# Smaller halves of a second fold by integer sum and difference on GpSimd, in 30 slots of a top-k attention and mixture-of-experts kernel

## The chip, the cores and the metric

The kernel runs on one core of a Trainium2 chip. The metric is device time in microseconds (us) of one execution; three executions of the kernel before gave 1314.14, 1318.43 and 1321.39, median 1318.43. The engines are named as in the profile: PE is TensorE, PEld its weight loads, DVE VectorE, ACT ScalarE, POOL GpSimd, SP the queue that issues most transfers.

## What is computed

Attention over 8 batches with 8 heads, 576 positions and head size 64, where each query keeps only its 32 best keys; then a mixture of experts with one expert out of 8 per token. All is float32.

```python
scores = scale * np.matmul(q, k.transpose(0, 1, 3, 2))
kth = np.partition(scores, -32, axis=-1)[..., -32:-31]
scores = np.where(scores >= kth, scores, -1e9)
...
attn = attn / (np.sum(attn, axis=-1, keepdims=True) + 1e-09)
x = np.matmul(attn, v)            # then heads side by side: 4608 rows of 512
...
h = np.maximum(x_sorted[lo:hi] @ w1[e], 0.0)
y_sorted[lo:hi] = h @ w2[e]
y = gate_w[:, None] * y[inv_perm]
```

## The kernel before

**Slots.** The attention goes in 144 slots, 18 to a batch. A slot holds two tiles of 128 query rows with 576 scores each, so 2 x 576 elements per partition. `loop()` writes out the order of PE, ACT and DVE by hand, slot after slot. Scores are made three to four slots ahead (`AHEAD`), so PE and ACT may lag behind DVE by some slots before it starves. Transposes and the product with V follow a slot later, and pieces of the expert blocks, planned by a credit that counts slots and not time, fill PE in between. From the first token rows that are ready (slot 25 on) expert blocks come in; what is left of them after the last slot is done by PE alone at the end.

**The search on DVE.** For the 32nd largest score of a row, DVE does not search all 576. `fold` (L313, L315) takes the larger and the smaller of column c and column c + 288: `h` and `l`. `fold_on` (L321, L323) does it again with `h`: the larger of each two go to `few[0:144]`, the smaller to `hl`, 144 wide. `search` first takes the eight largest of `l` and of the two halves of `hl` (L352, six MAX8 for two tiles) and puts them behind the 144 in `few`, which is then 168 wide. Four rounds then each take the eight largest (L361) and, but for the last, strike them out (L369). The first round needs the first 144 columns only. Round 0 strikes out in place in `few`; later ones write to `scr`. The order in DVE's queue in slot i is: `h` and `l` for slot i+1 (two-input TENSOR_TENSOR), the six lists for slot i, rounds 0, 1 and 2, then `few` and `hl` for slot i+1, then the last round. `h`, `hl` and `scr` have one buffer each, `few` three, `l` two.

**What follows it.** ACT turns the threshold into `low` (L378) and into `w` (L394); POOL subtracts (L403, two instructions for a slot), then writes a check value, `doubt` (L384); ACT takes the exponent (L411). Earlier in the slot, after round 0, POOL makes the bias of that exponent, `nbias` (L365). POOL works in order: L403 and L384 of slot i-1 come before L365 of slot i. In some slots it also scales finished rows (L496 to L509), scatters them (L574) or stores expert rows (L841), the last two as indirect transfers.

Of the kernel before, what the change touches and what calls it, by code (L numbers as in the profile page):

```python
# [9 lines left out]
F32 = mybir.dt.float32  # L10
I32 = mybir.dt.int32
AF = mybir.ActivationFunctionType
ALU = mybir.AluOpType
# [31 lines left out]
def kernel(  # L45
# [47 lines left out]
    nc = tc.nc  # L93
# [40 lines left out]
    def open_pools(st, exact):  # L134
        for name, bufs in (
            ("load", 2), ("att", 2), ("xp", 1 if exact else 2), ("small", 2),
            ("wp", 1 if exact else 2), ("mlp", 2),
        ):
            setattr(k, name, st.enter_context(tc.tile_pool(name=name, bufs=bufs)))
        for name, bufs in (("ps_s", 2), ("ps_t", 2), ("ps_m", 2)):  # L140
            pool = tc.tile_pool(name=name, bufs=bufs, space=bass.MemoryType.PSUM)
            setattr(k, name, st.enter_context(pool))
        k.exact = exact
        k.apart = k.between = False

    def load_unit(b, u, parts=False):
        n = SimpleNamespace(b=b, u=u)
# [167 lines left out]
        nc.vector.tensor_tensor(f.l, s[:, :, 0, :], s[:, :, 1, :], op=ALU.min)  # L315
        return f

    def fold_on(f):

        f.few = k.att.tile([P, 2, LW], F32, name="few", bufs=3)  # L320
        nc.vector.tensor_tensor(f.few[:, :, 0:QF], f.h[:, :, 0:QF], f.h[:, :, QF:HF], op=ALU.max)  # L321
        f.hl = k.att.tile([P, 2, QF], F32, name="hl", bufs=1)
        nc.vector.tensor_tensor(f.hl, f.h[:, :, 0:QF], f.h[:, :, QF:HF], op=ALU.min)  # L323

    aside = []

# [10 lines left out]
        if steps in aside:  # L337
            aside.remove(steps)

    def search(tiles, s, f, then=lambda: None):  # L340

        m_all = range(2)
        tops = k.small.tile([P, 2, TOP_K], F32, name="tops", bufs=4)
        if k.exact:
            src = [s[:, m, :, :].rearrange("p j k -> p (j k)") for m in m_all]
            width = S
        else:
            src = [f.few[:, m, 0:QF] for m in m_all]
            width = LW
            for m in m_all:  # L350
                for j, away in enumerate((f.l[:, m, :], f.hl[:, m, 0:QF // 2], f.hl[:, m, QF // 2:QF])):
                    nc.vector.max(out=f.few[:, m, QF + 8 * j:QF + 8 * j + 8], in_=away)  # L352
        scr = k.att.tile([P, 2, width], F32, name="scr", bufs=1)
        nbias = k.small.tile([P, 2], F32, name="nbias", bufs=3)
        R = TOP_K // 8

        for r in range(R):
            if r == R - 1:
                then()
            for m in m_all:  # L360
                nc.vector.max(out=tops[:, m, r * 8:(r + 1) * 8], in_=src[m])  # L361
                if r > 1:
                    tick()
            if r == 0:
                in_turn(nc.gpsimd.tensor_scalar_mul(nbias, tops[:, :, 0], -scale))  # L365
            if r < R - 1:
                for m in m_all:
                    first = r == 0 and not k.exact
                    nc.vector.match_replace(  # L369
                        out=src[m] if first else scr[:, m, :], in_to_replace=tops[:, m, r * 8:(r + 1) * 8],  # L370
                        in_values=src[m], imm_value=NEG,
                    )
                    if r > 1:
                        tick()
                    src[m] = f.few[:, m, :] if first else scr[:, m, :]
        thr = tops[:, :, TOP_K - 1]
        low = k.small.tile([P, 2], F32, name="low", bufs=3)
        nc.scalar.activation(low, thr, AF.Copy, scale=STEEP)  # L378

        def doubts():  # L380
            n, i = tiles[0]
            at = n.b * U + n.u
            over = doubt[:, at:at + 2, 2 * NC, :] if tails(tiles) else doubt[:, at, 2 * i:2 * i + 2, :]
            k.last_pool = in_turn(nc.gpsimd.tensor_tensor(  # L384
                over, f.few[:, :, QF + 7:LW:8], _inner(thr, NL), op=ALU.subtract
            )).ins

        return low, nbias, doubts
# [113 lines left out]

    def rows(n, x):

        rzb = rz_of[n.u % 2][:, :].rearrange("p (t h) -> p t h", h=2)
        at = 0 if n.u % 2 else lw
        xu = x[:, :, n.u * P:(n.u + 1) * P].rearrange("p t (h d) -> p t h d", h=2)
        xl = n.xl[:, :, at:at + P].rearrange("p t (h d) -> p t h d", h=2)
        in_turn(nc.gpsimd.tensor_tensor(xu, xl, _inner(rzb, D), op=ALU.mult))  # L509
# [453 lines left out]
    FIRST = 13  # L963
    ARRIVED = 13
    AHEAD = 3
    ON_CHIP = 3
    KEEP = 3 * PIECES
    BETWEEN = 2

    with fast:  # L970
# [39 lines left out]

        def put_stores():
            while stores:
                stores.pop(0)()

        def following():
# [29 lines left out]
        def scatter(n):  # L1045
            nonlocal left
            for _ in range(min(n, len(scatters))):
                scatters.pop(0)()
            if not scatters and coming:
                waiting.extend(coming)  # L1050
                left += len(coming) * PIECES
                coming.clear()
                ahead()
# [121 lines left out]
        def loop():  # L1175
            nonlocal credit, rate, clock
            for i in range(min(AHEAD, len(work))):
                multiply(i)
                s_of[i], steps = scores(got_of.pop(i))
                for step in steps:  # L1180
                    step()
            multiply(AHEAD)
            f_of[0] = fold(s_of[0])
            fold_on(f_of[0])
            for i, (b, g) in enumerate(work):
                tiles = tiles_of(i)
                u, tile = g[0]
                if tile == 0 and u % 2 == 0:
                    open_unit(tiles[0][0])
                if tails(tiles):  # L1190
                    open_unit(tiles[1][0])

                then = lambda: None
                if i + 1 < len(work):
                    f_of[i + 1] = fold(s_of[i + 1])
                    then = lambda: fold_on(f_of[i + 1])
                low, nbias, doubts = search(tiles, s_of[i], f_of.pop(i), then)
                at_place("small")
                w_of[i] = depths(s_of[i], low)
                less(s_of.pop(i), w_of[i])  # L1200
                doubts()
                at_place("pool")
                at_place("relu")
                at_place("rows")
                put_stores()
                scatter(1)
                at = i % per_batch
                if at == FIRST and b:
                    rate = level(b) * PIECES / (U * NT)
                credit += rate * len(g)  # L1210
                room = left
                if b == B - 1 and at >= ARRIVED:
                    room -= KEEP
                    credit = room / (len(work) - i)
                share = {0: 0.5, 1: 1.2, 2: 1.6, 3: 0.5, 2 * NC: 1.4}[tile]
                now = max(0, min(int(credit * share + 0.5), room))
                credit -= now
                clock = i
                if i + AHEAD < len(work):
                    s_of[i + AHEAD], steps = scores(got_of.pop(i + AHEAD))  # L1220
                    for step in steps:
                        step()
                evacuate()
                at_place("turn")
                turns = turning(i - 1) if i else iter(())
                next(turns, None)
                part = min(BETWEEN, now - now // 2)
                rest = pieces(part)
                next(turns, None)
                rest = pieces(now - now // 2 - part + rest)  # L1230
                weights(tiles, w_of[i], nbias)
                next(turns, None)
                evacuate()
                if i + AHEAD + 1 < len(work):
                    multiply(i + AHEAD + 1)
                if tile == NC - 1:
                    end = ending(b, u)
                    late.append([end, next(end)])
                at_place("products")
                at_place("weights")  # L1240
                credit = min(credit + pieces(now // 2 + rest), 6 * rate)

            k.between = True
            for _ in turning(len(work) - 1):
                pieces(1)
            assert len(late) == 1
            clock = None
            for place in late[0][0]:
                if place == "rows":
                    pieces(4)  # L1250
            kept = left - (SURE + HALVES + PLAIN) * PIECES
            assert kept >= 0, kept
            k.apart = True
            pieces(kept)
# [136 lines left out]
```

## Time and profile before

| what | value |
|---|---|
| the profiled execution's own time | 1319.47 us |
| its span | 1317.9 us, granted PE clock 0.965 |
| median of three runs | 1318.43 us (1314.14 to 1321.39) |
| busy, share of the span | PE 90%, DVE 81%, ACT 71%, POOL 50% |
| L403 on POOL | 288 instructions, 1434 ns each, 405.5 us idle before them |
| L323 on DVE (`hl`) | 144 instructions, 463 ns each |
| L321 on DVE (`few`) | 144 instructions, 550 ns each |
| mean device memory traffic | 168 GB/s |

A group's row gives the line, the engine, the operation, what it writes and reads, the count, then busy time and mean duration, then the idle time just ahead of it and who ended that. A timeline row gives start and duration in us; a bracket at its end is the idle time before it. Busy tenths are in 40 equal slices of the span, some 33 us each. On DVE an instruction's duration overlaps the next one by some hundredths, so the step from start to start says what it costs in a full queue.

### The profile page before, as it was taken

To read this page: it belongs to the slowest core of one execution; us is meant where nothing else is said; L and a number is where in the kernel's file an instruction comes from. 1 tells how busy PE (TensorE), PEld (TensorE's weight loads), DVE (VectorE), ACT (ScalarE), POOL (GpSimd) and SP (SyncE) were. 2 spreads that over 40 slices of the span, in tenths; PEclk is the share of its full clock that TensorE was granted. 3 is DMA by queue.
4 is the path that set the end of the run, shared out by engine and by line. 5 is a ranking of instruction groups with operands and counts; after the bars stand their busy time and mean duration, and the time that the engine had idled before them with its cause. 6 is when DMAs were issued, how large, how long until landed. Compare 5 with 4: busy or idle time off the path is not lost. (4 is left out here: it accounts for less than half of the span.)

```text
span 1317.9 us, 24504 instructions
## 1 busy us (share of the span) xinstructions
PE 1191.3 (90%) x7654; PEld 836.6 (63%) x7654; DVE 1069.2 (81%) x4617; ACT 931.7 (71%) x2136; POOL 662.0 (50%) x807
## 2 busy tenths in 40 slices
PE   5676777899889989999999999999999999999995
PEld 3343444655566556666666666667666777699973
DVE  8999999999999999999999999999999942000000
ACT  4788877888888887888788887898878851111110
POOL 2454546455755574658564745576558642000000
PEclk9788878999999999999999999999999999999998
DMA  4001013741473147434855554447454549986670
GB/s 149 29 30 30 30 38 102 267 161 39 137 265 140 46 156 282 174 110 148 299 173 182 166 210 173 165 150 292 145 204 149 205 154 311 378 284 212 212 291 18
DMA packets 98508, 220.94 MB, mean 168 GB/s; under 512 B 5181, under 2 KB 25917, under 8 KB 98368
## 3 DMA queue, kind: packets, MB, share of 16 engines
q1 hardware_dynamic: 91664, 199.02, 43.8%
q0 software_dynamic: 6416, 19.97, 4.2%
q8 instruction: 62, 1.02, 0.3%
q14 instruction: 78, 0.64, 0.2%
q10 hardware_dynamic: 288, 0.30, 0.1%
HBM read 195.88 MB, written 24.17 MB: 167 GB/s over the span
## 5 line engine op out<-in xcount | busy, mean ns | idle before, releaser
L403 POOL TENSOR_TENSOR w<-s,w 128x576 f32<-128x576 f32 x288 | 407.3, 1434 | 405.5 <-ACT w L394 405.4
L926 PE MATMUL ph<-xTs,w 128*128 128x128 f32 x2112 | 262.9, 279 | 5.1 <-ACT xTs L823 3.0
L926 PEld LDWEIGHTS ph<-xTs,w 128*128 128x128 f32 x2112 | 251.3, 194 | 24.3 <-issue 20.5
L943 PE MATMUL py<-w,hT 128*128 128x512 f32 x528 | 248.3, 599 | 3.9 <-ACT hT L931 3.7
L411 ACT ACTIVATE w<-w,nbias 128x576 f32<-128x576 f32 x288 | 224.1, 793 | 2.9 <-POOL w L403 2.2
L394 ACT ACTIVATE w<-s,low 128x576 f32<-128x576 f32 x288 | 207.6, 768 | 4.7
L299 PE MATMUL sc<-qkb 64*128 64x288 f32 (+1 forms) x1280 | 200.2, 463 | 9.4 <-ACT s L306 5.1
L422 PE MATMUL wTm<-turn,w 128*128 128x128 f32 x1152 | 166.9, 284 | 22.8 <-ACT xl L477 11.0
L422 PEld LDWEIGHTS wTm<-turn,w 128*128 128x128 f32 x1152 | 130.4, 144 | 79.7 <-issue 33.6
L306 ACT COPY s<-sc 128x576 f32<-128x576 f32 x288 | 168.7, 639 | 10.3 <-PE sc L299 10.3
L1270 DVE CAST any_i<-pd 1x1 int32<-1x1 f32 x1 | 0.1, 146 | 205.4 <-PE pd L1268 205.4
L361 DVE MAX8 tops<-scr 128x8 f32<-128x168 f32 x576 | 165.4, 315 | 0.0
L429 ACT COPY wT<-wTm 128x512 f32<-128x512 f32 x256 | 138.9, 603 | 23.8 <-PE wTm L422 23.7
L299 PEld LDWEIGHTS sc<-qkb 64*128 64x128 f32 (+1 forms) x1280 | 107.5, 191 | 70.0 <-issue 31.4
L361 DVE MAX8 tops<-few 128x8 f32<-128x144 f32 (+1 forms) x576 | 151.0, 300 | 0.0
L459 PE MATMUL po<-wT,vb 128*64 128x288 f32 x1024 | 150.0, 439 | 0.0
L943 PEld LDWEIGHTS py<-w,hT 128*128 128x128 f32 x528 | 91.9, 191 | 88.5 <-issue 82.6
L352 DVE MAX8 few<-l 128x8 f32<-128x288 f32 x288 | 127.1, 441 | 0.0
L841 POOL DMA_INDIRECT out_dram<-y,xg x37 | 38.9, 1052 | 173.5 <-ACT y L952 88.1
L459 PEld LDWEIGHTS po<-wT,vb 128*64 128x64 f32 x1024 | 72.5, 147 | 72.9 <-issue 21.6
L313 DVE TENSOR_TENSOR h<-s 128x576 f32<-128x576 f32 x144 | 109.3, 759 | 2.0 <-ACT s L306 2.0
L315 DVE TENSOR_TENSOR l<-s 128x576 f32<-128x576 f32 x144 | 108.6, 754 | 0.0
(188 smaller groups left out, 1654.5 us busy)
## 6 DMA issues: line engine op xcount, KB each, us to landing
w<-in_moe_w_dram SPq DMA_DIRECT2D x74, 2048.0 KB, 9.2
qkb<-in_qk_dram SPq DMA_DIRECT2D x31, 608.0 KB, 3.9
vb<-in_v_dram SPq DMA_DIRECT2D x32, 320.0 KB, 3.2
xg<-x_rows SPq DMA_DIRECT2D x37, 257.0 KB, 9.3
x_rows<-blank SPq DMA_DIRECT2D x13, 257.0 KB, 5.7
x_rows<-blank POOLq DMA_DIRECT2D x4, 257.0 KB, 9.7
x_rows<-x,posi POOLq DMA_INDIRECT x40, 3.5
out_dram<-y,xg POOLq DMA_INDIRECT x37, 4.1
```

Source lines behind the costliest of these rows:

```text
L299: nc.tensor.matmul(ps[rows, j, 0:HF], n.q[d, cols], n.k[d, keys], start=True, stop=True)
L306: lambda m=m, ps=ps: nc.scalar.copy(s[:, m, :, :], ps[:, :, 0:HF]) for m, ps in enumerate(got)
L352: nc.vector.max(out=f.few[:, m, QF + 8 * j:QF + 8 * j + 8], in_=away)
L361: nc.vector.max(out=tops[:, m, r * 8:(r + 1) * 8], in_=src[m])
L394: nc.scalar.activation(w[:, m, :], s[:, m, :, :].rearrange("p j k -> p (j k)"), AF.Relu, scale=-STEEP, bias=low[:, m:m + 1],)
L403: k.last_pool = in_turn(nc.gpsimd.tensor_tensor(w[:, m, :], s[:, m, :, :].rearrange("p j k -> p (j k)"), w[:, m, :], op=ALU.subtract)).ins
L411: nc.scalar.activation(w[:, m, :], w[:, m, :], AF.Exp, scale=scale, bias=nbias[:, m:m + 1], accum_out=n.z[:, c:c + 1])
L422: nc.tensor.transpose(pm[:, c * P:(c + 1) * P], w[:, m, first:first + P], ident)
L429: nc.scalar.copy(wT[:, :, m, q], pm4)
L459: nc.tensor.matmul(po[r, 0:HF], n.v[:, c, r], rhs, start=(c == 0), stop=(c == KC - 1))
L926: nc.tensor.matmul(ph[:, f, :], n.w1[:, 0, dt, fc * P:(fc + 1) * P], n.xT[:, dt, :], start=(dt == 0), stop=(dt == DT - 1),)
L943: nc.tensor.matmul(py, hT[:, f, :], n.w2[:, 0, f, :], start=(f == 0), stop=(f == FT - 1))
```

## The change

`fold_on` gets a second way to make `hl`: read as integers, the smaller of two numbers is their sum less the larger, and this is exact on the bits whatever they stand for. Two POOL instructions on int32 views (sum, then difference) take the place of one DVE minimum. It is used where a slot is "quiet": numbers 1 to 47, if no row scaling, scatter or store was queued since the last search. In the built program that is slots 1-7, 9-11, 13-16, 18-20, 22-24, 31-34, 36-38 and 40-42, that is 30. There `few` for the next slot comes already after round 1's maxima, ahead of round 1's strike-out, and POOL's two instructions stand in its queue behind `nbias` and ahead of L403 of the same slot. In a slot whose `hl` came from POOL the six lists come after round 0 instead of ahead of it.

```diff
-    def fold_on(f):
+    def fold_on(f, aside_too=False):
         f.few = k.att.tile([P, 2, LW], F32, name="few", bufs=3)
         nc.vector.tensor_tensor(f.few[:, :, 0:QF], f.h[:, :, 0:QF], f.h[:, :, QF:HF], op=ALU.max)
-        f.hl = k.att.tile([P, 2, QF], F32, name="hl", bufs=1)
-        nc.vector.tensor_tensor(f.hl, f.h[:, :, 0:QF], f.h[:, :, QF:HF], op=ALU.min)
+        hl = k.att.tile([P, 2, QF], I32, name="hl", bufs=1)
+        f.hl, f.aside = hl[:, :, :].bitcast(F32), aside_too
+        if aside_too:
+            one, other, more = (a.bitcast(I32) for a in (f.h[:, :, 0:QF], f.h[:, :, QF:HF], f.few[:, :, 0:QF]))
+            in_turn(nc.gpsimd.tensor_tensor(hl, one, other, op=ALU.add))
+            in_turn(nc.gpsimd.tensor_tensor(hl, hl, more, op=ALU.subtract))
+        else:
+            nc.vector.tensor_tensor(f.hl, f.h[:, :, 0:QF], f.h[:, :, QF:HF], op=ALU.min)
...
+    def lists(f):
+        for m in range(2):
+            for j, away in enumerate((f.l[:, m, :], f.hl[:, m, 0:QF // 2], f.hl[:, m, QF // 2:QF])):
+                nc.vector.max(out=f.few[:, m, QF + 8 * j:QF + 8 * j + 8], in_=away)
...
-            for m in m_all:
-                for j, away in enumerate(...)
+            if not f.aside:
+                lists(f)
...
-            if r == R - 1:
+            if r == R - 1 and not soon:
                 then()
...
+            if r == 1 and soon:
+                then()
...
+                if first and f.aside:
+                    lists(f)
...
+    QUIET = 48
...
-                then = lambda: None
+                then, quiet = lambda: None, 0 < i < QUIET and not k.crowded
                 if i + 1 < len(work):
                     f_of[i + 1] = fold(s_of[i + 1])
-                    then = lambda: fold_on(f_of[i + 1])
-                low, nbias, doubts = search(tiles, s_of[i], f_of.pop(i), then)
+                    then = lambda: fold_on(f_of[i + 1], quiet)
+                low, nbias, doubts = search(tiles, s_of[i], f_of.pop(i), then, quiet)
+                k.crowded = False
```

`k.crowded` is set to true where rows are scaled, stores are put out and rows are scattered.

More of the change, by code (lines that the diff above doesn't have):

```diff
@@ L143, in open_pools @@
         k.exact = exact
-        k.apart = k.between = False
+        k.apart = k.between = k.crowded = False
     def load_unit(b, u, parts=False):
@@ L338, in through, with search @@
             aside.remove(steps)
-    def search(tiles, s, f, then=lambda: None):
+    def lists(f):
+        for m in range(2):
+            for j, away in enumerate((f.l[:, m, :], f.hl[:, m, 0:QF // 2], f.hl[:, m, QF // 2:QF])):
+                nc.vector.max(out=f.few[:, m, QF + 8 * j:QF + 8 * j + 8], in_=away)
+    def search(tiles, s, f, then=lambda: None, soon=False):
         m_all = range(2)
@@ L349, in search @@
             width = LW
-            for m in m_all:
-                for j, away in enumerate((f.l[:, m, :], f.hl[:, m, 0:QF // 2], f.hl[:, m, QF // 2:QF])):
-                    nc.vector.max(out=f.few[:, m, QF + 8 * j:QF + 8 * j + 8], in_=away)
+            if not f.aside:
+                lists(f)
         scr = k.att.tile([P, 2, width], F32, name="scr", bufs=1)
@@ L503, in rows @@
     def rows(n, x):
+        k.crowded = True
         rzb = rz_of[n.u % 2][:, :].rearrange("p (t h) -> p t h", h=2)
@@ L1012, in put_stores @@
             while stores:
+                k.crowded = True
                 stores.pop(0)()
@@ L1047, in scatter @@
             for _ in range(min(n, len(scatters))):
+                k.crowded = True
                 scatters.pop(0)()
```

## The prediction

> **What bounds the kernel now.** First the busy tenths, since the change touches only the first 48 slots of 144, that is up to 354 us by the timeline.
>
> ```profile
> PE   5676777899889989999999999999999999999995
> ...
> DVE  8999999999999999999999999999999942000000
> ```
>
> DVE is full to slice 32, PE only from about slice 9 on. Next the busy time by stretches of 50 us:
>
> ```profile
> 50.00:100.00 50.00, 36.27 (x216) 21.35 (x216) 50.00 (x217) 42.01 (x101) 26.29 (x34) 0.86 0.12 39
> ...
> 300.00:350.00 50.00, 43.73 (x305) 28.77 (x302) 50.00 (x225) 41.66 (x101) 32.59 (x38) 1.00 0.18 59
> ...
> 1150.00:1200.00 50.00, 50.00 (x297) 46.75 (x296) 0.00 (x0) 7.84 (x13) 2.88 (x3) 1.00 0.73 252
> ```
>
> The numbers are PE, PEld, DVE, ACT, POOL. Up to 350 us DVE has no idle time at all and PE, ACT and POOL do. So a microsecond off DVE's queue there is a microsecond off the kernel, if nothing else becomes late. Afterwards PE binds, in an order fixed by slot; it starts from where DVE left it (up to slot 69, at 505 us, ACT still waits for DVE at nearly every `low`), so a lead made by slot 47 should last to the end. The chain of waits names no engine for the body and is of no use here.
>
> Then one slot on DVE, the one whose `h` starts at T = 80.72:
>
> ```profile
> 79.88 0.44 DVE L323 TENSOR_TENSOR hl<-h 128x288 f32<-128x288 f32 x1
> 80.24 0.56 DVE L361 MAX8 tops<-scr 128x8 f32<-128x168 f32 x2
> 80.72 0.73 DVE L313 TENSOR_TENSOR h<-s 128x576 f32<-128x576 f32 x1
> ...
> 84.28 0.55 DVE L361 MAX8 tops<-few 128x8 f32<-128x168 f32 x2
> ```
>
> And on POOL:
>
> ```profile
> 81.93 2.83 POOL L403 TENSOR_TENSOR w<-s,w 128x576 f32<-128x576 f32 x2 [3.75 <-ACT w L394]
> 84.72 0.20 POOL L384 TENSOR_TENSOR doubt<-few,tops 128x6 f32<-128x6 f32 x1
> 84.89 0.21 POOL L365 TENSOR_SCALAR nbias<-tops 128x2 f32<-128x2 f32 x1
> 89.42 2.79 POOL L403 TENSOR_TENSOR w<-s,w 128x576 f32<-128x576 f32 x2 [4.32 <-ACT w L394]
> ```
>
> POOL is idle from 85.10 to 89.42, and the next `h` starts at 87.71. A slot without other small work lasts 6.92 us from `h` to `h`, all of it DVE's.
>
> **Removed.** 30 L323. The row says 463 ns, but start to start (79.88 to 80.24) it costs 0.36. 30 x 0.36 = 10.8 us, the ceiling of the gain; 30 x 0.46 = 13.9 counts overlap twice.
>
> **Added on POOL.** An int32 TENSOR_TENSOR of 2 x 144 is nowhere in the trace. L403 (float32, 576) takes 1.41 in its median, L498 (40 elements) 0.27: on that line 288 take 0.80. Lower bound 0.68 (L509, 640 in 1.26, whose second input is broadcast), upper bound 1.41 (L403 whole, were integers twice as slow). I take 0.80, its nearest row in kind, so 1.6 plus about 0.08 between the two, as L498 and L499 show between dependent ones. The rule against this: the Trainium skill, GPSIMD Engine Reference, section "Engine selection", keeps elementwise work on VectorE, as GpSimd is about twice as slow with two inputs. The rows agree (1.41 against 0.73 for 576). Were POOL on the path, 30 x (1.68 - 0.36) = 40 us would be lost; the trace has POOL idle 4.3 us here, so by the row the two are hidden. That cover decides.
>
> **Who waits for them.** L403 of the slot is queued behind them: needed 1.2 us after the next T, so free. DVE's next `h` overwrites what the sum reads: done in time. The strike-out of round 0 now waits for the difference (it overwrites `few`): due 1.75 after the next T, so free; an extra semaphore at about 0.02 (the EVENT_SEMAPHORE row's 21 ns) makes 0.6 us in all. The lists wait for `hl` still later. That they and the maxima change places moves nothing on DVE's sum.
>
> **What moves: `few`, by 1.7 us.** This is where cost arises. A second view shows what happens when a two-input DVE instruction meets POOL:
>
> ```profile
> 515.79 2.79 POOL L403 TENSOR_TENSOR w<-s,w 128x576 f32<-128x576 f32 x2 [6.71 <-ACT w L394]
> 518.53 0.43 POOL L384 TENSOR_TENSOR doubt<-few,tops 128x6 f32<-128x6 f32 x1
> ```
>
> DVE at the same time:
>
> ```profile
> 517.40 1.50 DVE L321 TENSOR_TENSOR few<-h 128x288 f32<-128x288 f32 x1
> 518.82 0.45 DVE L323 TENSOR_TENSOR hl<-h 128x288 f32<-128x288 f32 x1
> ```
>
> `few` stood from 517.40 to 518.90, 1.06 longer than its 0.44, until POOL's subtraction was over. The Trainium skill, SBUF — State Buffer, section "Who interferes with whom", has it so: a VectorE instruction with two SBUF inputs and a GpSimd instruction that reads SBUF exclude each other for a whole instruction. MAX8 and MATCH_REPLACE rows, with one input, show no such stretch. Before, `few` came at 86.50, T + 5.78, clear of L403's end at T + 4.04. Now it comes when round 1's maxima end: 84.28 + 0.48, T + 4.04, in the very moment. On-time slots: at best no wait; at worst it stands behind `doubt` and `nbias`, 0.35. As the pending DVE instruction goes first in the view above (`doubt` is stretched, not `few`), I take 0.1: 24 x 0.1 = 2.4 us.
>
> Late slots: where ACT is behind, L403 ends later. In slot 11 (T = 87.71) `low` is not preceded by idle time, L403 ends at T + 4.50, and with ACT's slack cut by 0.3 a slot at T + 4.8: `few` loses 0.7. Doing this for every quiet slot (ACT's work from `low` to `low` less its idle time, against the shorter slot) gives 0.25, 0.3, 0.45 and 0.25 in slots 15, 24, 34 and 42. In slot 40 row scaling left over from slot 39 holds L403 until T + 5.49: `few` can slip in between its two instructions, but then the difference runs into the next `h`, about 0.7. Together 2.7 us.
>
> **Does POOL get done?** From the start of `few`, DVE goes 2.52 us to the next `h` (0.37 + 0.60 + 0.47 + 0.60 + 0.48). POOL needs the rest of `few` 0.4, `nbias` 0.25, sum and difference 1.68, less some 0.1 at the end: 2.23. It fits with 0.29 to spare, which allows 0.94 an instruction.
>
> Sum: -10.8 + 0.6 + 2.4 + 2.7 = -5.1. The profiled execution's 1319.5 becomes 1314.4. That execution is 1.0 above the median, so in runs 1313.3.
>
> **Rivals.**
> 1. *Integers are slow* (slower). The place is the next `h`, held by the difference. Each 0.1 over 0.94 an instruction costs 0.2 a slot; from about 1.12 on that eats the 0.36. A stalled `h` gives L403 the lead it lacked, so `few`'s waits are left out. At the bound, 1.41, `h` waits 0.93: (0.93 - 0.36) x 30 + 0.6 = +18, 1336; at 1.27 it waits 0.65: +9, 1328, which I take. Against it: 128-lane rows with two inputs lie on one line whatever they do. 15%.
> 2. *No collisions*: `few` wins the tie and ACT, which waits inside its slots for PE too, keeps up. -10.8 + 0.6 = -10.2: 1308. 22%.
> 3. *POOL wins the tie*: `doubt` and `nbias` go ahead each time, 0.25 in 24 slots: -10.8 + 0.6 + 6.0 + 2.7 = -1.5: 1317. 15%.
> 4. *The lead is lost behind slot 47*, PE's work from 520 us on having its own pace. Against it: ACT's waits for DVE up to slot 69. 1318. 8%.
>
> My own case has 40%.
>
> **The numbers.** 0.5% is 6.6 us, about what a measurement of this kernel can tell from no change. Faster by more: rival 2 and 30% of my case, 0.34. Slower by more: rival 1 mostly, 0.13. Within: 0.53. The range: 1308 (rival 2) to 1321 (my case and rival 3 with the 2.6 us by which the runs of before stand from their median on either side, and short of rival 1).
>
> **What would show it.** L323 on DVE x114; two new POOL groups x30 near 800 ns (over 1100: rival 1); L313 unstretched in slots 1 to 47 (median 0.73); L321's total up by about 4.4 us, its mean from 550 to about 580 ns; ordinary quiet slots of 6.6 to 6.7 us in place of 6.92; and slot 48's `h` at about 349, not 354. If slot 48 comes early and the end does not, rival 4 holds.

## The result, and the profile after

The changed kernel takes 1313.03 us in the median of 18 runs (1311.18 to 1316.37), the kernel before 1318.64 in 18 (1314.14 to 1321.65). The ratio is 0.996, with a 95% interval of 0.9951 to 0.9968: by the ratio 5.3 us faster, between 4.2 and 6.5. The medians here and below leave out two executions that ran in a far slower state, one of the kernel with the minimum left out (1725.94 us, granted PE clock 0.651) and one of the kernel before (1730.48 us). Forecast were 1313.3 and a gain of 5.1 us, so the size came out to within a tenth of a per cent of the whole. By its steps the forecast was less good: one cost that it counted is not there, and another is larger.

The page of the changed kernel, its busy tenths:

```profile
PE   5776676899889989999999999999999999999995
...
DVE  7999999999999999999999999999999943000000
ACT  4888877898888888988888887898878851111210
POOL 4777766777755575658564745576558542000000
```

DVE is still full, and POOL's slices two to eight have gone from four to six tenths to six or seven. By stretches of 50 us (PE, PEld, DVE, ACT, POOL):

```profile
50.00:100.00 50.00, 37.16 (x225) 22.52 (x225) 49.76 (x210) 43.05 (x103) 36.48 (x46) 0.86 0.12 39
300.00:350.00 50.00, 43.95 (x308) 29.68 (x306) 49.91 (x220) 42.54 (x101) 38.30 (x41) 1.00 0.20 64
...
1150.00:1200.00 50.00, 50.00 (x318) 49.45 (x318) 0.00 (x0) 9.44 (x15) 2.72 (x3) 1.00 0.75 266
```

In the first of these POOL is busy for 36 us where it was for 26. The groups that answer to the rows of before (POOL's new pair, `few`, the minimum that is left on DVE, the check value):

```profile
L321 DVE TENSOR_TENSOR few<-h 128x288 f32<-128x288 f32 x144 | 80.8, 561 | 0.0
...
L329 DVE TENSOR_TENSOR hl<-h 128x288 f32<-128x288 f32 x114 | 53.3, 467 | 0.0
...
L399 POOL TENSOR_TENSOR doubt<-few,tops 128x6 f32<-128x6 f32 x144 | 45.4, 315 | 0.0
...
L327 POOL TENSOR_TENSOR hl<-hl,few 128x288 int32<-128x288 int32 x30 | 24.4, 815 | 2.4
L326 POOL TENSOR_TENSOR hl<-h 128x288 int32<-128x288 int32 x30 | 23.8, 794 | 0.0
```

The integer instructions take 794 and 815 ns, against 800 forecast from the float32 rows. `few` is only 11 ns longer in the mean; `doubt` is 63 ns longer (it took 36.3 us in all before). How that comes shows in an ordinary slot, T = 24.41. POOL:

```profile
25.62 2.83 POOL L418 TENSOR_TENSOR w<-s,w 128x576 f32<-128x576 f32 x2 [1.41 <-ACT w L409]
28.41 0.54 POOL L399 TENSOR_TENSOR doubt<-few,tops 128x6 f32<-128x6 f32 x1
28.92 0.21 POOL L378 TENSOR_SCALAR nbias<-tops 128x2 f32<-128x2 f32 x1
29.09 0.79 POOL L326 TENSOR_TENSOR hl<-h 128x288 int32<-128x288 int32 x1
29.97 0.80 POOL L327 TENSOR_TENSOR hl<-hl,few 128x288 int32<-128x288 int32 x1
```

and DVE:

```profile
28.45 0.44 DVE L321 TENSOR_TENSOR few<-h 128x288 f32<-128x288 f32 x1
28.81 0.08 DVE L382 MATCH_VALUE_LOAD scr<-tops,few 128x8 f32 x1
...
30.96 0.74 DVE L313 TENSOR_TENSOR h<-s 128x576 f32<-128x576 f32 x1
```

`few` starts 0.04 after `doubt` and takes its bare 0.44; it is `doubt` that stands, 0.54 in place of 0.20. So the tie goes to DVE, at no cost, and in no ordinary quiet slot of this profile is `few` stretched. The difference ends at 30.77, 0.19 ahead of the next `h`. The slot lasts 6.55 us, not 6.92: 0.37 less, all of the step that was removed.

A late slot is number 6, T = 50.62. POOL, then DVE:

```profile
53.14 2.76 POOL L418 TENSOR_TENSOR w<-s,w 128x576 f32<-128x576 f32 x2 [2.72 <-ACT w L409]
55.86 0.42 POOL L399 TENSOR_TENSOR doubt<-few,tops 128x6 f32<-128x6 f32 x1
```

```profile
54.66 1.57 DVE L321 TENSOR_TENSOR few<-h 128x288 f32<-128x288 f32 x1
56.14 0.08 DVE L382 MATCH_VALUE_LOAD scr<-tops,few 128x8 f32 x1
```

`low` came 1.4 us after T, so POOL's subtraction ends at 55.9, and `few` stands from 54.66 until then: 1.1 us lost in a slot that saves 0.37.

**A trap in the first profile of before.** Taken against it, slot 48 began only 2.3 us early, though the span is 7.1 us shorter. One slot that the change does not touch, number 26, lasts 11.95 us in the changed kernel and 8.72 there. A second profile of before (the first experiment below) lasts 11.57 in it:

```profile
201.93 0.15 DVE L638 TENSOR_TENSOR past<-slots,upto_max 1x24 f32<-1x24 f32 x1
202.01 0.32 DVE L361 MAX8 tops<-scr 128x8 f32<-128x168 f32 x1
202.26 4.16 DVE L643 TENSOR_TENSOR past<-past,step_all 1x24 f32<-1x24 f32 x1
206.35 0.74 DVE L313 TENSOR_TENSOR h<-s 128x576 f32<-128x576 f32 x1
```

An instruction on 24 numbers, 0.15 us in the first profile, stands for 4 us, as POOL works from 202.15 to 206.3 without a gap:

```profile
202.15 0.26 POOL L501 TENSOR_TENSOR lg<-xl 128x40 f32<-128x40 f32 x1
202.38 1.25 POOL L509 TENSOR_TENSOR x<-xl,rz 128x640 f32<-128x640 f32 x1
203.60 2.76 POOL L403 TENSOR_TENSOR w<-s,w 128x576 f32<-128x576 f32 x2
206.32 1.50 POOL L384 TENSOR_TENSOR doubt<-few,tops 128x6 f32<-128x6 f32 x1
```

In the first profile another small instruction (L638) had met the row scaling ahead of this one, stood 1.37 us behind it alone, and the long stand did not come. Against the second profile of before, whose span is 1316.2, slot 48 begins 5.6 us early in the changed kernel, the last slot's `h` 5.9 and the span ends 5.4 early. All leads below are taken against this second profile. That of the kernel with a third POOL instruction (8.65 in slot 26) is the only other one without the long stand, so its lead in the table is some 3 us higher than with it.

### The profile page after: what moved, and what is told of

Its sections match the earlier page's. It is cut to its first block, busy times and chain, and to the rows that moved or that the text cites. A ratio compares the mean times of both kernels' runs of the same rounds, so it can differ in the third digit from the quotient of the medians.

```text
span 1310.7 us, 24598 instructions
## 1 busy us (share of the span) xinstructions
PE 1184.7 (90%) x7654; PEld 830.4 (63%) x7654; DVE 1064.8 (81%) x4587; ACT 931.8 (71%) x2136; POOL 715.4 (55%) x867
## 5 line engine op out<-in xcount | busy, mean ns | idle before, releaser
L418 POOL TENSOR_TENSOR w<-s,w 128x576 f32<-128x576 f32 x288 | 406.9, 1433 | 345.3 <-ACT w L409 345.2
L942 PE MATMUL ph<-xTs,w 128*128 128x128 f32 x2112 | 259.6, 276 | 3.3 <-ACT xTs L839 3.0
L942 PEld LDWEIGHTS ph<-xTs,w 128*128 128x128 f32 x2112 | 248.0, 192 | 22.5 <-issue 18.7
L299 PE MATMUL sc<-qkb 64*128 64x288 f32 (+1 forms) x1280 | 196.8, 459 | 9.5 <-ACT s L306 5.1
```

What stands on the lines that cost most here:

```text
L299: nc.tensor.matmul(ps[rows, j, 0:HF], n.q[d, cols], n.k[d, keys], start=True, stop=True)
L418: k.last_pool = in_turn(nc.gpsimd.tensor_tensor(w[:, m, :], s[:, m, :, :].rearrange("p j k -> p (j k)"), w[:, m, :], op=ALU.subtract)).ins
L942: nc.tensor.matmul(ph[:, f, :], n.w1[:, 0, dt, fc * P:(fc + 1) * P], n.xT[:, dt, :], start=(dt == 0), stop=(dt == DT - 1),)
```

## The experiments

Medians and intervals are those of each experiment's own comparison with the kernel before (5 to 12 executions each, 18 of the changed kernel). The lead is how much earlier slot 48 begins.

| kernel | median, us | ratio to before (95%) | lead at slot 48, us |
|---|---|---|---|
| changed kernel, first profile | 1313.03 | 0.996 (0.9951 to 0.9968) | 5.6 |
| changed kernel, second profile | one run, 1313.4 | | 5.8 |
| minimum left out | 1307.91 | 0.993 (0.9916 to 0.9943) | 9.8 |
| POOL's pair left out | 1311.30 | 0.9953 (0.9939 to 0.9967) | 6.9 |
| order alone | 1319.83 | 1.0007 (0.9995 to 1.0019) | -2.4 |
| pair in the old place | 1319.52 | 1.0006 (0.9997 to 1.0016) | -1.4 |
| a third POOL instruction | 1325.44 | 1.0054 (1.0037 to 1.007) | -3.8 |
| one round later | 1314.04 | 0.9965 (0.9951 to 0.9979) | 3.8 |
| up to slot 70 | 1313.14 | 0.996 (0.9945 to 0.9975) | 4.1 |
| without slots 6, 11, 34, 40 | 1313.83 | 0.9966 (0.9955 to 0.9978) | 4.1 |

**The kernel before, again.** No edit.

> The kernel before once more, for a second profile of it. All five profiles with another order in the first 48 slots lose about 3 us in slot 26 (a small DVE instruction stands 4.16 us behind POOL) and win 1.6 us back in slots 70 to 76; the one profile of before does neither. Theory: that profile is the odd one, a chance of timing, and this one shows the 12 us in slot 26 too; then the lead at slot 48, measured against it, is about 5.5 us and not 2.3. Rival: before never has it and the change brings it about: slot 26 stays at 8.7 us.

11.57 us in slot 26, so the rival falls. The expectation said that all five profiles with another order show it; one taken beside this run then did not. The same kernel has it in one profile and not in another, so it is chance of timing, and a lead of one profile against one other may not be read to better than some 3 us.

**The changed kernel, again.** No edit.

> The changed kernel once more, for a second profile of it. In its first profile slot 48 began only 2.3 us early, as one slot (number 26, which the change does not touch) lost 3.2 us to a small DVE instruction that stood 4.16 us behind POOL, and PE was late in slots 6 and 11. If this is chance of timing (my theory: PE runs at half clock in spells of 3.4 us and more in the first 250 us, and which slots these hit decides which slots are late), the slots that lose time differ in this profile, slot 48 begins 2 to 7 us early, and ordinary quiet slots stay at 6.55 us. If the loss belongs to the change (rival), slot 26 takes about 12 us again and slots 6 and 11 are late again.

Slot 26 takes 12.02 us again (see above: before has it too). Ordinary slots last 6.55. Of the quiet slots, 6, 11, 15, 20, 22, 33, 34 and 41 fall short of the full 0.37 in both profiles, but by other amounts: 1.14 and 0.35 us in slot 6, 0.20 and 0.66 in slot 33. So which slots are late is mostly fixed by the kernel, and how late is not. PE's granted clock fits that, shown by two stretches around slots 4 to 6 and 10 to 11 (last numbers: clock, transfer share, GB/s), first the changed kernel, then before:

```profile
37.20:57.50 20.30, 14.59 (x76) 8.41 (x77) 20.30 (x86) 16.41 (x37) 14.62 (x20) 0.75 0.09 32
78.20:91.60 13.40, 11.18 (x78) 6.10 (x80) 13.40 (x61) 10.54 (x25) 8.86 (x12) 0.88 0.22 71
```

```profile
37.20:57.50 20.30, 12.92 (x70) 7.66 (x70) 20.30 (x88) 16.07 (x37) 9.62 (x13) 0.84 0.10 32
78.20:91.60 13.40, 11.89 (x79) 6.11 (x75) 13.40 (x60) 9.79 (x25) 5.35 (x6) 0.82 0.15 50
```

The clock differs from one profile to the next in the same place. In slot 6 the rest of the chain can be read off ACT, ahead of the late `low`, in the first and then in the second profile of the changed kernel:

```profile
48.02 0.41 ACT L476 COPY oT<-po 128x288 f32<-128x288 f32 x1 [2.16 <-PE po L474]
```

```profile
47.12 0.40 ACT L476 COPY oT<-po 128x288 f32<-128x288 f32 x1 [1.36 <-PE po L474]
```

ACT waits 0.80 us longer for PE in the first, and that is the whole difference between 1.14 and 0.35. PE's granted clock in the 24 us ahead of the slot was 0.57 in the first and 0.72 in the second. That the clock is why PE was late is argued; no run here changed the clock alone. It isn't the reason everywhere: slot 41 loses its 0.63 in both profiles at a granted clock of 1.00.

**The minimum left out.** The 30 slots read other columns in place of `hl`, and POOL gets nothing new; all else as before.

```diff
         if aside_too:
-            one, other, more = (a.bitcast(I32) for a in (...))
-            in_turn(nc.gpsimd.tensor_tensor(hl, one, other, op=ALU.add))
-            in_turn(nc.gpsimd.tensor_tensor(hl, hl, more, op=ALU.subtract))
+            f.hl, f.aside = f.l[:, :, 0:QF], False
...
-                low, nbias, doubts = search(tiles, s_of[i], f_of.pop(i), then, quiet)
+                low, nbias, doubts = search(tiles, s_of[i], f_of.pop(i), then, False)
```

> In the 30 slots the smaller halves of the second fold are not made at all: the lists read the first 144 columns of the first fold's smaller halves in their place, so the output is another one. The order on DVE is that of before, POOL gets nothing new. Theory (a DVE step of 0.36 us is removed 30 times, and what is missing from 10.8 us is waits of few behind POOL): ordinary slots 6.56 us, no new stretched few, slot 48 about 10.8 us early, the time near 1308, ratio 0.992. Rival (the gain comes from few and the lists changing place): no more than 1318. Rival (the lead is lost behind slot 47): slot 48 10.8 us early and the end not, 1313 or more.

1307.91, just under the 1308 expected; the last `h` begins 10.2 us early and the span is 10.3 us shorter. The ordinary slot lasts 6.55, no quiet slot loses any of its 0.37, and what is missing from 30 x 0.37 = 11.1 lies in slots that are not quiet (8, 17, 19, 26, 30, 35 and 43 are longer by 0.2 to 0.55). The removal is worth what its start-to-start step says, and a lead made in the first 48 slots is there at the end, so both rivals fall. That holds for this lead of 10 us; a lead of 3 us between the two profiles of before did not last (see the end).

**The order alone.** `few` early and the lists late; the minimum stays on DVE, behind `few`.

```diff
         if aside_too:
-            one, other, more = (...)
-            in_turn(nc.gpsimd.tensor_tensor(hl, one, other, op=ALU.add))
-            in_turn(nc.gpsimd.tensor_tensor(hl, hl, more, op=ALU.subtract))
+            nc.vector.tensor_tensor(f.hl, f.h[:, :, 0:QF], f.h[:, :, QF:HF], op=ALU.min)
```

> few early and the lists late as in the changed kernel, but the minimum stays on DVE, right behind few; POOL gets nothing new. Theory: ordinary quiet slots back at 6.92 us, and the late slots still lose what few, and now the minimum too, waits behind L403: 2 to 6 us slower than before, 1321 to 1325. Rival (the new order is what gains): near 1313, as fast as the changed kernel.

1319.83, which cannot be told from before: less than the 2 to 6 us expected, 1321 to 1325, and so a miss in size. In the profile it is 2.4 us behind at slot 48 and 2.1 at the end. The rival falls. Ordinary slots last 6.92, and slots 6, 11, 20, 33 and 34 are longer by 0.2 to 1.0 us, each with a stretched `few` behind L403.

**POOL's pair left out.** As the changed kernel, `few` early; the lists read other columns in place of `hl`.

```diff
-            in_turn(nc.gpsimd.tensor_tensor(hl, one, other, op=ALU.add))
-            in_turn(nc.gpsimd.tensor_tensor(hl, hl, more, op=ALU.subtract))
+            f.hl = f.l[:, :, 0:QF]
```

> As the changed kernel, few early and the lists late, but POOL's two instructions are left out and the lists read the first fold's smaller halves in place of hl, so the output is another one. It parts what is missing from the full gain (1308.6 without the minimum at all, 1313 in the changed kernel) into two. Theory: the waits of few behind a late L403 cost about 2 us (the kernel with the order alone lost 1 to 2), so about 1310.5; the other 2 to 3 us come from the pair itself, which pushes h, l and few of the next slot in late slots. Rival (few's waits are all of it): 1313. Rival (few's waits cost nothing): 1308.5.

1311.30, between. From the minimum left out to this, early `few` costs 3.4 us by the medians and 2.9 by the lead; from this to the changed kernel, the pair costs 1.7 by the medians and 1.1 to 1.3 by the lead. The intervals of neighbours overlap, so the two shares are not exact, but that both have a part is borne out by where they lie: here slots 6, 11, 20, 33 and 34 lose 2.8 us in `few`; in the changed kernel `l` of slot 12 and `h` of slot 41 stand behind the difference as well (0.61 and 0.51 us).

**The pair in the old place.** `few` and POOL's two instructions ahead of the last round.

```diff
-                low, nbias, doubts = search(tiles, s_of[i], f_of.pop(i), then, quiet)
+                low, nbias, doubts = search(tiles, s_of[i], f_of.pop(i), then, False)
```

> Sum and difference on POOL as in the changed kernel, but few and these two stand in the old place, ahead of the last round; the lists are late. Theory: few comes at T + 5.35 and POOL's two instructions last until about T + 7.1, past the next h at T + 6.55, which must wait for the sum to be complete and for the shared reads, and the strike-out of round 0 for the difference: each quiet slot loses 0.1 to 0.6 us more than the 0.36 it saves is worth, so 1318 to 1328, with h or l or the strike-out late in ordinary slots. Rival (place is of no account, POOL's idle time takes it anywhere): 1308 to 1313.

1319.52: the gain is gone. In an ordinary slot POOL comes to the difference 1.17 us later than it could, and `h` stands behind it (POOL, then DVE):

```profile
29.04 0.79 POOL L326 TENSOR_TENSOR hl<-h 128x288 int32<-128x288 int32 x1
31.00 0.80 POOL L327 TENSOR_TENSOR hl<-hl,few 128x288 int32<-128x288 int32 x1 [1.17 <-DVE few L321]
```

```profile
31.26 1.15 DVE L313 TENSOR_TENSOR h<-s 128x576 f32<-128x576 f32 x1
32.34 0.75 DVE L315 TENSOR_TENSOR l<-s 128x576 f32<-128x576 f32 x1
```

1.15 in place of 0.73: 0.42 us lost for 0.37 saved; slots of 6.97. Of the mechanism expected, the reads that exclude each other are there. The sum is early and `h` waits for it no longer, as the sum needs `h` only; that part was wrong.

**A third POOL instruction.** The sum is made twice.

```diff
             in_turn(nc.gpsimd.tensor_tensor(hl, one, other, op=ALU.add))
+            in_turn(nc.gpsimd.tensor_tensor(hl, one, other, op=ALU.add))
             in_turn(nc.gpsimd.tensor_tensor(hl, hl, more, op=ALU.subtract))
```

> A third POOL instruction in each of the 30 slots: the sum is made twice (the same value). Theory (POOL's reads and DVE's two-input instructions share one way into memory, and an ordinary slot of 6.55 us is full of them: h, l and few 1.7, L403 2.8, doubt and nbias 0.4, sum and difference 1.6): the difference now ends at T + 7.2, and h, or few of the next slot, loses 0.4 to 0.8 us in each ordinary slot: 7.0 to 7.3 us, slower than before, 1321 to 1332. Rival (POOL's idle time has room for more): 1313 to 1315, ordinary slots at 6.55.

1325.44, 7 us slower than before and 12 slower than the changed kernel. POOL and DVE in an ordinary slot:

```profile
29.73 0.79 POOL L326 TENSOR_TENSOR hl<-h 128x288 int32<-128x288 int32 x1
30.59 0.80 POOL L327 TENSOR_TENSOR hl<-h 128x288 int32<-128x288 int32 x1
31.46 0.79 POOL L328 TENSOR_TENSOR hl<-hl,few 128x288 int32<-128x288 int32 x1
32.80 2.00 POOL L419 TENSOR_TENSOR w<-s,w 128x576 f32<-128x576 f32 x1 [0.55 <-ACT w L410]
```

```profile
31.59 1.28 DVE L313 TENSOR_TENSOR h<-s 128x576 f32<-128x576 f32 x1
32.80 0.75 DVE L315 TENSOR_TENSOR l<-s 128x576 f32<-128x576 f32 x1
```

`h` takes 1.28 in place of 0.74, and the slot lasts 7.1. POOL stands idle for half a microsecond ahead of L419 all the same. So POOL's idle time is not by itself room. `h` does not need what L328 makes or reads, yet it stands until L328 is over at 32.25. A budget fits that: in the changed kernel h, l and few take 1.7 us of a slot of 6.55, POOL's readers 2.8 + 0.4 + 1.6 = 4.8, and that is 6.5. It is a rough one, since with the third instruction it makes 7.3 where the slot lasts 7.1.

**One round later.**

```diff
-            if r == 1 and soon:
+            if r == 2 and soon:
```

> few and POOL's two instructions one round later, after the maxima of round 2, so that few comes at T + 5.1 and a late L403 that ends by then no longer holds it. Theory: ordinary quiet slots at 6.55 to 6.65 (sum is made before few, difference after it, to T + 6.4), late slots lose less to L403 but some to the sum, which now stands in the way of few, and to h behind the difference: within 3 us of the changed kernel, 1310 to 1316. Rival (the waits behind L403 are the whole of what is missing from 10.8 us): 1308.

1314.04, as good as the changed kernel within the interval. Slots 15 and 42 lose 0.6 and 0.8 us with `few` behind the sum, slots 7 and 40 with `l` or `h` behind the difference. The waits change place and not their sum, so the rival falls.

**Up to slot 70.**

```diff
-    QUIET = 48
+    QUIET = 70
```

> The bound of 48 slots set to 70, which adds the quiet slots among 48 to 69. DVE is full there too and ACT still waits for it in most slots, but PE is 93 to 98% busy. Theory: ordinary quiet slots there drop to 6.55 at first, ACT and PE fall behind in some, L403 comes late and few waits: a gain of 0 to 4 us on the changed kernel, 1309 to 1313. Rival (PE sets the pace from slot 48 on, leads are lost): the lead at slot 69 is not above that at slot 48, 1313 or more.

1313.14, no gain on the changed kernel. The lead does grow from slot 48 to 69, by 1.6 us, where eleven slots at 0.37 would make 4.1; most of the rest is lost to slot 58, longer by 1.1 with `few` stretched, and slot 61, longer by 0.7. Its lead at slot 48 was 1.5 us smaller, mostly in slot 40, which lasts 8.49 us in this profile, with the same instructions up to there as in the changed kernel, where it lasts 7.19 and 7.18: chance again. Whether the 1.6 are worth anything stays open: intervals of 2 us on either side cannot tell.

**Without slots 6, 11, 34 and 40.**

```diff
+    LATE = (6, 11, 34, 40)
...
-                then, quiet = lambda: None, 0 < i < QUIET and not k.crowded
+                then, quiet = lambda: None, 0 < i < QUIET and not k.crowded and i not in LATE
```

> The changed kernel with slots 6, 11, 34 and 40 taken out of the 30: in its two profiles these, with the slot behind them, lost more than the 0.37 us they save. Theory (which slots are late is partly a matter of PE's clock, but these four carry the most ACT work or the leavings of row scaling, so most of it stays): 1 to 2 us better than the changed kernel, 1311 to 1312.5. Rival (the lateness just moves to the slots behind them): 1313 to 1314.

1313.83, no better, as the rival had it: slots 9, 15, 20, 33 and 36, of which 9 and 36 were not late before, now lose 0.6 to 0.75 us each. But slot 40, taken out, lasts 8.52 us here with an `l` stretched by 1.07, near the 8.49 of the run above, so part of the smaller lead is that, and the profile alone does not show that the lateness only moved. No version was found that beats the changed kernel beyond doubt.

## Why the prediction was right, point by point

- **What is removed, 10.8 us.** Right: 0.37 a slot measured, 10.2 us at the last `h` with nothing in its place.
- **Size of the integer instructions, 0.80 us.** Right (0.79 and 0.82), and so rival 1 fell. That it would have gone as priced is shown by the third POOL instruction, which has the same place and, at 0.8 us more on POOL, a stand of 0.55 at `h`; priced at 1.2 us an instruction, rival 1 would have had 0.52.
- **The cover on POOL.** Right that the pair is hidden in an ordinary slot; 0.29 us to spare were forecast, of which 0.1 was taken off POOL's work at its end; without that it is 0.19, and 0.19 from record to record are there. The Trainium skill's rule (GPSIMD Engine Reference, section "Engine selection") that elementwise work belongs on VectorE would, with the two instructions on the path, have made a loss of 40 us by the prediction's estimate; measured is a gain of 5.3, since the longer work lies beside DVE and not on it.
- **On-time slots, 2.4 us for `few`.** Mis-sized: it is nothing. The reason given, that DVE's pending instruction goes first, holds fully (`doubt` 0.54). The 0.6 us for semaphores are not there either: the slot gives back all of its 0.37. `few`'s total rose by 1.6 us (79.2 to 80.8) and its mean to 561 ns, not by 4.4 and to 580.
- **Late slots, 2.7 us in slots 11, 15, 24, 34, 40 and 42.** Mechanism right, size short. Against the second profile of before, quiet slots lost 4.2 us. In slots 11, 15 and 34, and in 41 where slot 40's cost lands, that is 2.3, against 2.1 forecast for these four; slots 24 and 42 lost nothing of their 0.55. Slot 40 went as described: `few` slips in between L418's two instructions, and the difference runs into the next `h`:

```profile
300.00 0.79 POOL L327 TENSOR_TENSOR hl<-hl,few 128x288 int32<-128x288 int32 x1
```

```profile
300.16 1.25 DVE L313 TENSOR_TENSOR h<-s 128x576 f32<-128x576 f32 x1
```

  That is 0.51 of the 0.7 forecast. Not forecast were slots 6, 20, 22 and 33, 1.9 us together, and four slots that are not quiet, another 2.05 (number 12 with `l` behind the difference 0.6, 17 with `few` behind row scaling 0.4, 26 and 43 with 0.4 and 0.7). The weak step is "ACT's work from `low` to `low`", taken from one profile as if it were the kernel's own: slot 6, the largest, lost 1.14 in one profile and 0.35 in the next. Slots that are not quiet were put at nothing. And "done in time" for the sum failed in slot 11, where the next `h` waited 0.24 us for it.
- So 3.0 us of cost that was not there and 3.5 that was not counted nearly cancel, with 0.3 more removed than forecast: -11.1 + 4.2 + 2.05 = -4.9, with 0.5 us of difference from other slots of the profile of before making the 5.4 read between slots 1 and 48. The total was better than its terms, and that it came within 0.3 us was luck.
- **Rival 2, 22%.** Its place was right for the tie and wrong for late slots; the kernel with the minimum left out is what it described, 1307.9. **Rival 3** falls with the tie. **Rival 4** falls: 5.6 us at slot 48, 5.4 at the end, and the medians of 18 runs say 5.3.

## What to carry to other kernels

An engine's idle time is not room for another instruction if that instruction and those of the engine it is to relieve exclude each other: add up, slot by slot, the two-input DVE instructions and the reading POOL ones, and see whether the sum fits the slot that is to come out. That is needed and not enough: with the same sum in the old place the slot lasted 6.97 us and not 6.55. A step taken out of a full queue is worth its start-to-start interval, not its duration, and a step moved earlier has to be set against the late cases of what it now meets, not the mean one. Before a difference of a few microseconds between two profiles is explained, take the old kernel's profile twice.

## What the runs showed that was not expected

A DVE instruction that stands behind POOL usually gets in as soon as POOL's running instruction is over (`few` at 54.66, `doubt` waiting for it). The one in slot 26 did not: it stood for 4.16 us through L501, L509 and two L403 in a row, and it stands in ten of the twelve profiles, of before and of changed kernels alike. Its size, 24 elements on one partition, is one difference, but no run tried it, and what decides which small instruction meets the row scaling was not tried either. Nor did the 3 us of this stand reach the end: the first profile of before, without it, leads the second by 3.3 us at slot 48 and by 2.1 at the last `h`, and its span is 1.7 us longer, since what comes after the last `h` takes 267.6 us in place of 263.9. In the other eleven profiles that tail lasts 263.8 to 265.5. Why that one tail is some 4 us longer stays open.
